# A new issue order for every engine of a one-core attention-plus-spectral-filter kernel

## The chip, the core and the metric

The kernel runs on one core of one Trainium2 chip. The metric is the device time of one execution in microseconds (us); lower is better. A core has five engines that run their own instruction streams and meet only at semaphores: TensorE (PE, matrix products into PSUM), VectorE (DVE), ScalarE (ACT), GpSimd (POOL) and SyncE (SP, which here only issues transfers). In the profile PEld is the loading of a matmul's stationary operand, a name ending in q is an engine's instruction queue.

## What is computed

Two token mixers over the same input, added under a gate per token. Branch A is attention in four segments of 512 tokens with a running memory; branch B is a filter in the frequency domain. Cut to what matters:

```python
B, S, D, H, N, L = 1, 2048, 640, 32, 4, 512        # head width Dh = 20
g = sigmoid((x * gate_w).sum(-1, keepdims=True))
q, k, v = x @ wq, x @ wk, x @ wv                    # as heads and segments
for s in range(N):
    p = softmax(qs @ ks.T * Dh**-0.5 + causal_mask)
    a_mem = (phi(qs) @ M) / (phi(qs) @ z + 1e-6)    # phi(t) = t+1 if t>0 else exp(t)
    out_s = gh * a_mem + (1 - gh) * (p @ vs)        # gh = sigmoid(beta), per head
    M, z = M + phi(ks).T @ vs, z + phi(ks).sum()
a = concat(out_s) @ wo
b = irfft2(rfft2(x) * (w_r + 1j * w_i))
return g * a + (1 - g) * b
```

## The kernel before

Everything is cut to 128 partitions. `record` writes the computation down as 2328 operations, each with what it reads and writes; a second table, `ORDER`, says in which order every engine issues them; `schedule` turns both into instruction streams and chooses buffers, and `emit` puts the waits in. One entry of `ORDER` holds an operation and the engine that does it:

```python
for v in order:
    o = ops[v // 2]
    o.eng = list(o.alts)[v % 2]
    queue[o.eng].append(o)
```

So an entry's half is the operation's number, and an odd entry takes the second of its two engines, where it has two. Each engine keeps its queue strictly: an instruction that waits holds up all that stand behind it on that engine. Which operation may run on which engine is fixed where it is recorded. Copies out of PSUM (`copy_alts`, L519) go to ScalarE or VectorE. [...] Products by the PSUM operand are VectorE's alone.

PSUM has eight banks. Four belong to the scores of attention (`qk`, one unit fills all four); the other four (`gen`) are handed round among all other matmul groups. A group takes a bank with its first matmul, and the bank is free for another when the operation that reads it out has ended. Since a group is often the fifth that wants one, a matmul often waits for an eviction.

The steps, with the lines they have in the profile:

- Opening. Transposed loads of x (`xt_load`, profile line L546), loads of the weights and of x in the filter's layout (L548). A first product of four heads (`proj_direct`) and the projections of q, k, v follow; all matmuls show as L514 (L512 where one product is split into four column groups). `fold` (L901, L906) adds and subtracts halves of x for the filter, on VectorE or GpSimd.
- Attention, segment by segment. `qk_unit` makes the scores, ScalarE takes their exponential (L1263, tile ex), GpSimd zeroes what the causal mask hides (L1284), a product with v follows. 80 such score units run one after the other through the whole kernel, and all other work lies between them.
- Memory. `phi` is made by L1072 (ACT) and L1084, L1085 (DVE); `mem_read_tile` divides the memory's answer (L1152, L1155, L1157; L1160 in the last segment).
- Filter. Products with tables, a product by the filter (L1439), sums (L1444), products back, and sums into the tile G (L1485).
- Denominators, for segments 0 to 2. `denominators` (L1202) reads the sums of the softmax back from DRAM, inverts them (L1211), multiplies them by the gate (L1213, tile rc), stores them (r_scr) and `finish_tile` loads them again spread over partitions (tile r), where five products with the attention output need them (L1526, `normal`, tile oU).
- Finish. Four tiles for each segment (`finish_tile`, L1506). For segments 1 and 2 the memory's part is loaded (tile mT, a transposing load) and added (L1534, `addmem`, 128x640). Then the filter's last product and the product with wo go into one bank, the bank is read out (L523 on ACT, L525 on DVE, tile ot) and stored.

TensorE works in three shapes: the full array; four row groups, for the scores (`qk`); four column groups, for half of the v products, the products of probabilities and v in segments 0 to 2, and the finish. A group of one shape that follows a group of another is called a change of shape below.

Of the kernel before, what the change touches and what calls it, by code (L numbers as in the profile page):

```python
# [461 lines left out]
class Kern:  # L462
# [79 lines left out]
    def dma(self, dst, src, nbytes, r, w, prio, tr=False, name="", after=(), queue="sp"):  # L542
# [37 lines left out]
        46, 0, 90, 26, 74, 23, 2, 4, 36, 24, 6, 8, 28, 10, 12, 72, 14, 16, 30, 18, 20, 178, 64, 34, 202, 66, 68, 44, 42, 70, 93, 214, 52, 190, 48, 94,  # L580
        204, 97, 216, 180, 192, 218, 104, 98, 182, 76, 206, 101, 194, 38, 208, 220, 196, 103, 198, 222, 201, 184, 224, 186, 210, 188, 296, 50, 212,
        256, 298, 362, 78, 300, 536, 32, 80, 274, 538, 258, 83, 302, 260, 262, 276, 130, 278, 264, 84, 54, 280, 106, 266, 282, 1904, 86, 304, 364,
        284, 88, 366, 108, 380, 306, 576, 132, 826, 268, 290, 828, 814, 110, 368, 578, 831, 816, 113, 382, 384, 386, 819, 370, 540, 388, 832, 270,
        834, 410, 412, 272, 836, 414, 416, 391, 418, 552, 372, 490, 420, 288, 492, 494, 114, 496, 498, 554, 118, 820, 822, 134, 336, 500, 240, 137,
        338, 242, 340, 120, 348, 58, 824, 342, 116, 350, 308, 122, 312, 544, 142, 226, 932, 546, 124, 344, 292, 244, 56, 228, 144, 246, 286, 248, 347,
        139, 352, 230, 294, 232, 126, 250, 354, 146, 234, 374, 1906, 149, 237, 1908, 356, 254, 1910, 359, 2094, 151, 238, 1912, 844, 1914, 252, 2124,
        140, 2126, 1916, 2128, 128, 2130, 360, 166, 2096, 40, 846, 2098, 154, 2132, 848, 2100, 2134, 1924, 326, 1926, 314, 2102, 168, 392, 1928, 2104,
        1930, 156, 892, 310, 1932, 152, 838, 1944, 1934, 170, 334, 1946, 158, 894, 840, 324, 316, 1948, 842, 808, 897, 161, 328, 810, 1950, 1952, 394,
        320, 813, 880, 886, 163, 882, 322, 1954, 888, 560, 332, 502, 884, 504, 396, 506, 330, 172, 508, 890, 448, 376, 510, 1936, 398, 450, 436, 512,
        438, 378, 402, 452, 514, 562, 440, 174, 442, 2162, 400, 1962, 2164, 176, 444, 2166, 516, 556, 454, 456, 2168, 446, 165, 2170, 458, 464, 460,  # L590
        466, 406, 1918, 468, 462, 470, 570, 472, 408, 2172, 910, 912, 542, 474, 898, 900, 318, 914, 602, 903, 2150, 548, 604, 2152, 2154, 2156, 2158,
        1920, 2178, 572, 404, 2160, 1966, 2180, 1958, 2182, 1922, 1968, 574, 904, 60, 2184, 2174, 2186, 906, 594, 2188, 1956, 564, 908, 1970, 2176,
        580, 934, 874, 596, 876, 1972, 879, 476, 566, 1974, 62, 478, 480, 550, 1977, 868, 870, 930, 422, 568, 482, 424, 873, 484, 426, 928, 916, 558,
        486, 428, 430, 488, 918, 2136, 432, 598, 2138, 920, 2140, 434, 2142, 856, 582, 858, 1960, 2144, 922, 519, 861, 924, 606, 584, 2146, 936, 1938,
        520, 2148, 926, 588, 523, 1020, 525, 608, 586, 652, 591, 2596, 802, 654, 862, 850, 804, 864, 852, 1940, 2216, 867, 2204, 2206, 2218, 2208,
        2220, 1942, 2210, 2222, 1980, 854, 2224, 2212, 656, 634, 2226, 2214, 1978, 778, 658, 2006, 2228, 636, 780, 2230, 2008, 1982, 2190, 2010, 782,
        2012, 526, 946, 2014, 786, 784, 2192, 948, 1964, 938, 940, 942, 2194, 788, 950, 2196, 945, 2198, 952, 600, 660, 2017, 2200, 790, 662, 2202,
        792, 2018, 976, 978, 1984, 794, 2020, 958, 798, 796, 1986, 960, 980, 954, 2233, 800, 1988, 982, 610, 956, 664, 2038, 612, 1990, 528, 2236,
        2234, 1992, 965, 530, 984, 986, 2040, 1995, 534, 2076, 988, 2078, 962, 2042, 1996, 2000, 1998, 2044, 991, 614, 618, 1016, 2080, 2024, 620,
        2002, 996, 1014, 2082, 2238, 638, 998, 2084, 972, 2004, 2022, 2046, 622, 668, 974, 992, 624, 2086, 2049, 2056, 626, 1018, 994, 1070, 1072,  # L600
        2058, 1074, 666, 2060, 1022, 1076, 642, 1002, 2050, 806, 1104, 1024, 1026, 670, 645, 1001, 2062, 532, 1028, 2270, 2064, 1031, 628, 2036, 2636,
        2252, 2240, 1106, 2272, 630, 2638, 2274, 2254, 640, 2066, 2276, 2106, 676, 616, 2640, 2256, 678, 592, 2258, 1010, 1004, 2243, 2026, 966, 968,
        2052, 2070, 2028, 1013, 632, 692, 971, 1006, 694, 680, 2244, 2642, 1009, 2644, 686, 1032, 2068, 1034, 682, 2246, 646, 1100, 2054, 2090, 1036,
        2030, 2088, 684, 2288, 649, 710, 2034, 2646, 672, 2290, 1039, 2566, 712, 674, 2292, 2598, 2294, 2600, 2306, 2072, 2602, 2110, 2604, 2308,
        2606, 2074, 2568, 2310, 700, 2092, 2108, 2312, 714, 2608, 726, 2112, 2786, 703, 716, 728, 2114, 1044, 2788, 2570, 688, 1062, 1064, 1046, 2790,
        696, 1066, 2792, 2794, 2650, 1069, 690, 1040, 2796, 650, 2574, 734, 1042, 1110, 698, 1078, 736, 1108, 1082, 730, 1080, 1112, 1114, 1118, 1102,
        1120, 732, 1122, 1116, 750, 1084, 1124, 2260, 2032, 738, 752, 2278, 1049, 2578, 2262, 2280, 2264, 2580, 2282, 704, 2266, 1051, 2284, 2268,
        2296, 2582, 744, 706, 1148, 1150, 2298, 718, 2586, 2648, 754, 2300, 1058, 720, 2302, 3288, 1152, 1089, 2616, 1061, 2618, 1126, 1155, 740,
        1130, 1052, 746, 1132, 1054, 2620, 2572, 1056, 2332, 1086, 1204, 1128, 748, 1206, 2334, 1208, 2622, 2624, 2250, 756, 1096, 1211, 1090, 1135,
        1192, 1092, 2627, 762, 2118, 1095, 2576, 2610, 2390, 1194, 1137, 1098, 1196, 765, 1198, 2392, 1200, 2314, 2120, 2698, 1203, 722, 2700, 2628,  # L610
        1138, 2316, 2702, 2318, 742, 1156, 2122, 1158, 2320, 1160, 1140, 724, 708, 1163, 2704, 2630, 2324, 2612, 2116, 1142, 1168, 2654, 2614, 2706,
        770, 2326, 1170, 1164, 758, 1166, 2842, 2844, 2846, 2848, 761, 2850, 2658, 2652, 2328, 2364, 2852, 766, 2676, 2330, 2366, 2709, 2678, 1280,
        2660, 2584, 2680, 2662, 2712, 2590, 1175, 2870, 2664, 1278, 2592, 2666, 2632, 2682, 2656, 2668, 2348, 1190, 2684, 2634, 2350, 2854, 2336,
        2710, 2856, 2858, 2860, 2862, 2672, 2286, 2896, 2687, 2898, 2864, 2358, 2340, 2866, 2872, 1274, 2352, 2868, 2342, 2874, 2876, 2360, 2882,
        2816, 768, 2884, 2818, 2362, 2878, 2820, 2688, 2886, 2880, 2888, 2822, 2890, 1188, 2692, 2824, 2690, 2900, 2344, 2826, 2902, 2904, 2670, 2382,
        2368, 2828, 2892, 2384, 2830, 2894, 2832, 2346, 2748, 2834, 2906, 2750, 1242, 2370, 1244, 1246, 2752, 2674, 2836, 2376, 2694, 1248, 2716,
        2838, 2696, 2448, 2714, 772, 2338, 2754, 2354, 2450, 2730, 2732, 2356, 2840, 2734, 2736, 2756, 1173, 2738, 2372, 2741, 2758, 2386, 2422, 2588,
        2378, 2375, 1144, 2760, 2394, 1176, 2742, 1147, 2768, 1186, 2770, 2424, 2718, 2772, 2322, 2774, 2802, 2776, 2744, 1178, 2764, 3290, 2779,
        2594, 1234, 3292, 1236, 774, 1238, 2798, 2762, 2746, 2406, 2782, 3328, 1276, 1241, 2408, 3294, 3296, 2766, 3298, 2720, 3330, 2780, 3301, 1182,
        2416, 2398, 1184, 3332, 1181, 2418, 2400, 1212, 2728, 3334, 2784, 3336, 1214, 2420, 1216, 2908, 2910, 2410, 1218, 3308, 3338, 2402, 2912,  # L620
        2440, 2800, 2404, 1254, 2442, 1250, 2426, 1256, 3310, 3312, 3314, 3316, 1252, 2428, 2914, 2916, 2412, 2434, 2918, 3318, 2804, 1366, 2498,
        1222, 2920, 1220, 1282, 2806, 2500, 2922, 2925, 1224, 2444, 1284, 2437, 3258, 2414, 1286, 3260, 1289, 1226, 2396, 1272, 1320, 1322, 3262,
        2927, 1290, 1292, 1229, 2304, 1324, 2388, 2506, 1326, 1294, 3266, 2952, 2508, 2380, 2446, 2962, 1297, 2430, 3320, 2954, 2964, 1259, 2956,
        2966, 3270, 3340, 2968, 3272, 2502, 2248, 2958, 3322, 1328, 2452, 2464, 3274, 2944, 2433, 2466, 1330, 2454, 3278, 2504, 3282, 2946, 1332,
        2948, 2456, 3284, 4010, 1334, 2468, 2950, 1298, 2458, 1260, 1362, 2980, 3350, 1300, 2470, 3352, 1302, 2474, 4008, 3354, 1304, 1230, 2476,
# [981 lines left out]
```

## Time and profile before

| | us |
|---|---|
| median of 13 runs | 244.34 |
| lowest, highest | 242.32, 245.25 |
| the profiled execution | 244.84 |
| its span, first to last instruction | 242.9 |
| mean granted TensorE clock | 0.993 of full |

| engine | busy us | share | instructions |
|---|---|---|---|
| PE | 227.3 | 94% | 4347 |
| ACT | 199.6 | 82% | 241 |
| DVE | 197.0 | 81% | 481 |
| POOL | 166.6 | 69% | 297 |

The profiled execution took 244.84 us, 1.9 more than its span, and 0.5 more than the median of the runs. Busy time of an engine is the time in which at least one of its instructions was under way; matmuls overlap, so PE's share says that it seldom stood still and not that it ran at its peak. The transfers moved 42.17 MB, 174 GB/s on the mean.

### The profile page before, as it was taken

The numbers are of one execution on the slowest core, as the hardware profiler recorded it, in microseconds if no ns is written. First come the engines' busy times: TensorE is split into PE (matmuls) and PEld (weight loads), VectorE is DVE, ScalarE is ACT, GpSimd is POOL, SyncE is SP. The second block draws the span as 40 slices with busy tenths as digits, with TensorE's granted clock in tenths as the row PEclk, the third lists the DMA queues.
The fourth block names the chain that finished last, engine by engine and source line by source line (L and its number), as shares of the span: only waits on it lengthen the run. The fifth ranks groups of instructions, "written<-read, shape, count | busy, mean of one in ns | idle before, by whom it ended". The sixth has DMA issues, their size and how long they took to land.

```text
span 242.9 us, 10242 instructions
## 1 busy us (share of the span) xinstructions
PE 227.3 (94%) x4347; PEld 141.2 (58%) x4361; DVE 197.0 (81%) x481; ACT 199.6 (82%) x241; POOL 166.6 (69%) x297
## 2 busy tenths in 40 slices
PE   7799999999999999999989999899989999799994
PEld 2575567665556565555546555455545557467794
DVE  0579998789899986997999798997988887736563
ACT  2189688799899999999989979999899978488730
POOL 8524268457969956947964999876899867559730
PEclk9999999999999999999999999999999999799999
DMA  7999849996996775494787572364776997642123
GB/s 171 279 363 213 227 123 165 268 205 148 244 233 155 169 227 144 106 232 92 237 205 236 167 217 66 101 171 139 189 217 200 221 198 83 125 71 85 57 86 108
DMA packets 58928, 42.17 MB, mean 174 GB/s; under 512 B 30020, under 2 KB 55172, under 8 KB 58884
## 3 DMA queue, kind: packets, MB, share of 16 engines
q1 hardware_dynamic: 57844, 40.96, 69.4%
q8 instruction: 34, 0.56, 1.0%
q10 hardware_dynamic: 1040, 0.57, 0.8%
q14 instruction: 10, 0.08, 0.1%
HBM read 23.32 MB, written 12.30 MB: 147 GB/s over the span
## 4 chain that ended last, share of the span: by engine, by line
PE 49%; DVE 20%; DMA 11%; ACT 9%; SPq 6%; issue 3%; ACTq 0%; DVEq 0%
PE psum L514 44%; ACT ex L1263 6%; PE psum L512 5%; SPq L548 3%; SPq L546 3%; DMA xsb<-in_A_x_dram 3%; DMA r_scr<-rc 3%; DMA qkp<-qk_scr 2%; DVE xf L901 2%; DVE xsb L906 2%; DMA qk_scr<-qu 2%; DVE Pt L1439 2%; DVE G L1485 1%; DVE va L1115 1%; DVE oU L1526 1%
## 5 line engine op out<-in xcount | busy, mean ns | idle before, releaser
L1263 ACT ACTIVATE ex<-psum 128x2048 bf16<-128x2048 f32 (+4 forms) x92 | 138.7, 1507 | 13.9 <-PE psum L514 12.3
L1284 POOL TENSOR_SCALAR_AFFINE_SELECT ex<-ex 128x256 bf16<-128x256 bf16 (+2 forms) x224 | 122.0, 567 | 40.0 <-ACT ex L1263 36.5
L514 PE MATMUL psum<-qkp 20*64 20x64 bf16 (+5 forms) x1280 | 32.6, 271 | 2.9 <-ACT ex L1263 1.9
L514 PE MATMUL psum<-xT,wk 128*128 128x256 bf16 (+1 forms) x280 | 34.0, 273 | 0.8 <-DMA wk<-in_A_wk_dram 0.6
L514 PE MATMUL psum<-wv,xT 128*32 128x321 bf16 (+3 forms) x400 | 30.0, 301 | 0.3 <-DVE va L1115 0.2
L514 PE MATMUL psum<-xT,wq 128*128 128x512 bf16 (+1 forms) x121 | 27.0, 380 | 1.5 <-DMA xT<-in_A_x_dram 0.8
L1439 DVE TENSOR_TENSOR Pt<-psum,Wt 128x642 bf16<-128x642 f32 x32 | 25.6, 822 | 2.3 <-PE psum L514 1.9
L514 PEld LDWEIGHTS psum<-qkp 20*64 20x64 bf16 x1280 | 13.5, 103 | 20.2 <-ACT ex L1263 13.5
L514 PEld LDWEIGHTS psum<-xT,wk 128*128 128x128 bf16 (+1 forms) x280 | 19.9, 97 | 6.9 <-DMA wk<-in_A_wk_dram 0.9
L512 PE MATMUL psum<-wo,oU 128*32 128x320 bf16 x480 | 22.7, 310 | 0.0
L906 POOL TENSOR_TENSOR xsb<-xf 128x320 bf16<-128x320 bf16 (+2 forms) x12 | 9.4, 788 | 16.7 <-DVE xsb L906 12.5
L525 DVE CAST ot<-psum 128x320 bf16<-128x320 f32 x21 | 10.1, 491 | 11.3 <-PE psum L512 8.9
L514 PEld LDWEIGHTS psum<-wv,xT 128*32 128x32 bf16 (+1 forms) x400 | 14.6, 96 | 7.9 <-issue 2.4
L1115 DVE TENSOR_TENSOR va<-psum,ebx 128x320 bf16<-128x320 f32 x32 | 15.2, 483 | 4.7 <-ACT gate L1113 2.4
L514 PE MATMUL psum<-big,Ac 128*128 128x160 bf16 (+2 forms) x96 | 18.1, 258 | 0.7 <-DVE Pt L1439 0.3
L514 PE MATMUL psum<-big,Cp 128*128 128x321 bf16 (+1 forms) x96 | 18.0, 302 | 0.2 <-DVE G L1485 0.2
L514 PE MATMUL psum<-ex,va 128*32 128x64 bf16 (+3 forms) x576 | 17.4, 256 | 0.7 <-DVE dn L1152 0.3
L1485 DVE TENSOR_TENSOR G<-eo,psum 128x320 bf16<-128x320 f32 x32 | 14.7, 482 | 3.6 <-PE psum L514 2.6
L514 PE MATMUL psum<-tt,Yt 128*128 128x256 bf16 (+1 forms) x96 | 16.4, 275 | 0.4 <-ACT qu L523 0.3
L514 PEld LDWEIGHTS psum<-ex,va 128*32 128x32 bf16 x576 | 11.0, 96 | 9.7 <-POOL ex L1284 3.4
L1072 ACT ACTIVATE et<-qu 128x512 bf16<-128x512 bf16 x25 | 15.6, 629 | 0.2
L512 PEld LDWEIGHTS psum<-wo,oU 128*32 128x32 bf16 x480 | 12.4, 99 | 4.8 <-issue 1.1
(99 smaller groups left out, 392.7 us busy)
## 6 DMA issues: line engine op xcount, KB each, us to landing
qkp<-qk_scr SPq DMA_DIRECT2D x28, 160.0 KB
tt<-tab_tt SPq DMA_DIRECT2D x8, 512.0 KB, 4.4
qk_scr<-qu SPq DMA_DIRECT2D x12, 256.0 KB, 3.6
u_scr<-ub SPq DMA_DIRECT2D x12, 256.0 KB, 3.6
xsb<-in_A_x_dram SPq DMA_DIRECT2D x8, 320.0 KB, 6.8
oU<-u_scr SPq DMA_DIRECT2D x15, 128.0 KB, 3.3
out_dram<-ot SPq DMA_DIRECT2D x12, 160.0 KB
Wt<-in_B_w_r_dram SPq DMA_DIRECT2D x16, 80.2 KB, 2.6
```

The source lines that it names most:

```text
L512: h = e.matmul(dst, wt, r_, start=st, stop=sp_, **{**kw, "tile_position": (0, q), "skip_group_check": True})
L514: h = e.matmul(o_, l_, r_, start=st, stop=sp_, **kw)
L525: alts["dve"] = (lambda e: e.tensor_copy(dst(), src()), 67 + 1.04 * n, 68.0)
L546: return e.dma_start_transpose(d_, s_)
L548: return e.dma_start(d_, s_)
L906: self.either(lambda e, dst=dst, src=src, d0=d0, n=n, op=op: e.tensor_tensor(xs.ap(o + dst, [D, 2], [1, n]), xf.ap(src + d0, [321, 2], [1, ...
L1072: self.one("act", lambda e: e.activation(et.ap(0, [1, L]), qsl(), ACT.Exp), L, [qb], [b("et", pi_)], late, name="phi_exp")
L1115: self.one("dve", lambda e: e.tensor_tensor(va.ap(i * H * VW + h0 * VW, [VW, nh], [1, DH]), self.ps(bank, 0, [DH, nh], [1, DH]), self.ebx. ...
L1263: self.one("act", lambda e, d=d, q=q: e.activation(self.ex.ap(*d), self.ps(bank, *q), ACT.Exp, scale=SC), n, [bank], [self.exb(s, 2 * pr + ...
L1284: self.one("pool", lambda e: e.affine_select(self.ex.ap(e0 + d0, [1280, 4], [1, n], np_=np_), self.ex.ap(e0 + s0, [1280, 4], [1, n], np_=np_),
L1439: self.one("dve", lambda e, ri=ri, Pt=Pt, Wt=Wt, wo_=wo_, bank=bank: e.tensor_tensor(Pt.ap(ri * 322, [644, 2], [1, KD]), self.ps(bank, 0, ...
L1485: self.one("dve", lambda e, q=q, n2=n2, bank=bank, eo=eo: e.tensor_tensor(self.G.ap(n2 * D + 639 * q, [1 - 2 * q, 320]), eo.ap(q, [1, 320] ...
```

## The change

Only the table `ORDER` differs; the operations, their buffers' sizes and the scheduler are the same. The first and the last rows of it:

```diff
     ORDER = (
-        46, 0, 90, 26, 74, 23, 2, 4, 36, 24, 6, 8, 28, 10, 12, 72, 14, 16, 30, 18, 20, 178, 64, 34, 202, 66, 68, 44, 42, 70, 93, 214, 52, 190, 48, 94,
-        204, 97, 216, 180, 192, 218, 104, 98, 182, 76, 206, 101, 194, 38, 208, 220, 196, 103, 198, 222, 201, 184, 224, 186, 210, 188, 296, 50, 212,
...
+        23, 0, 104, 24, 90, 72, 2, 26, 4, 6, 8, 28, 10, 12, 14, 74, 16, 46, 30, 202, 18, 34, 190, 44, 178, 20, 48, 180, 52, 192, 92, 42, 182, 95, 214,
+        194, 216, 204, 96, 218, 206, 36, 196, 208, 38, 198, 210, 201, 220, 212, 222, 184, 98, 186, 100, 188, 296, 32, 225, 103, 274, 298, 256, 76,
...
```

The built programs show what the new table moves. TensorE has the same 1073 matmul groups with the same 80 score units in the same sequence, the groups between them in a new one; changes of shape go from 229 to 241. Operations that change engine, net:

| operation | before | after |
|---|---|---|
| copies out of PSUM on ACT (L523) | 93 | 98 |
| of these the last ones (tile ot) | 11 | 17 |
| `fold` on POOL | 16 | 12 |
| `normal` on POOL (L1526) | 2 | 0 |
| `addmem` on POOL (L1330, L1534) | 5 | 2 |
| filter sums on POOL (L1444) | 16 | 15 |
| gate tables on POOL (L1022) | 2 | 4 |
| small gate operations on POOL | 11 | 15 |

Four places that the prediction speaks of, in the order of the built streams ("|" stands between instructions, numbers in brackets are operation numbers):

```
SP, opening
before  x part 1 | xT chunk 0 | beta | wk | xT chunks 1-2 | xT chunks 3-4 | wk rest | x part 0 | ...
after   wk | xT chunk 0 | xT chunks 1-2 | x part 1 | xT chunks 3-4 | wk rest | x part 0 | ...

DVE, memory read of segment 2
before  mem_den | gate | mem_rec | phi_max(1652) | mem_den | mem_rec | mem_mul(1493)
after   mem_den | mem_mul | mem_rec | W_mul | mem_mul(1493) | mem_den | mem_rec | phi_max(1652)

DVE, denominators of segment 2
before  ... sum, sum | gate table | sum, sum | L1211(1626) | normal, sum, sum | L1213(1627)
after   ... sum, sum | sum | last eviction | sum | L1211(1626) | L1213(1627)

finish of segment 2, its first tile: DVE  L1526 x5 | rs | addmem(2080) | rs | on(1915), in both
POOL beside it   before  addmem(2178), 128x640      after  addmem(2129), 128x640 | addmem(1865), 128x320
DVE further on   before  on | addmem(1865)          after  sum | addmem(2178)
```

## The prediction

> **What bounds the kernel now.** I read the page first (busy times, slices), then who waited for whom, the stretches of 1 us around the largest stop, and the timelines of the engines there.
>
> ```profile
> span 242.9 us, 10242 instructions
> PE 227.3 (94%) x4347; PEld 141.2 (58%) x4361; DVE 197.0 (81%) x481; ACT 199.6 (82%) x241; POOL 166.6 (69%) x297
> ...
> PEclk9999999999999999999999999999999999799999
> ```
>
> TensorE is the bound: it stands still for 242.9 - 227.3 = 15.6 us, of which 1.3 lie before its first matmul and 3.1 behind its last. Within the busy time lie the changes of shape. In the trace's list of weight loads, four-column groups of 320 columns start 136 ns apart; before a group of another shape the distance is 371, and that group's next follows after 15 instead of 136. A change of shape thus costs (371 - 136) - (136 - 15) = 114 ns, and 229 of them 26 us.
>
> ```profile
> PEld psum L514 <- ACT ex L1263: 13.5, 44, 0.8
> PEld psum L514 <- POOL ex L1284: 3.9, 12, 0.5
> PEld psum L514 <- DVE Pt L1439: 3.7, 15, 0.6
> ...
> PEld psum L514 <- DVE on L1325: 1.8, 1, 1.8
> PEld psum L514 <- DVE mem L1157: 1.8, 3, 1.3
> ```
>
> The columns are total, times, longest. Most stops are many and short: weight loads held until a score bank or a general bank is read out. They are spread over the kernel and no single edit takes them away. Two are long, the last two rows. The first of these, in stretches (busy PE, PEld, DVE, ACT, POOL; then the granted clock):
>
> ```profile
> 206.00:207.00 1.00, 0.69 (x28) 0.59 (x24) 0.96 (x4) 0.97 (x2) 0.79 (x1) 1.00 0.56 56
> 207.00:208.00 1.00, 0.00 (x0) 0.00 (x0) 1.00 (x2) 0.47 (x1) 0.60 (x1) 1.00 0.27 97
> ...
> 210.00:211.00 1.00, 1.00 (x20) 0.62 (x16) 0.47 (x1) 0.97 (x2) 0.68 (x3) 0.50 0.52 150
> ...
> 212.00:213.00 1.00, 1.00 (x22) 0.37 (x15) 0.85 (x3) 0.44 (x1) 0.00 (x0) 0.50 1.99 165
> ```
>
> TensorE stops at 206.7, goes on at 208.4, and from about 210 to 213 the granted clock is 0.50. Why it stopped, from three engines' timelines:
>
> ```profile
> 204.05 2.01 DVE L1526 TENSOR_TENSOR oU<-oU,r 128x512 bf16<-128x512 bf16 x5 [0.89 <-DMA r<-r_scr]
> 206.21 1.39 POOL L1534 TENSOR_TENSOR oU<-oU,mT 128x640 bf16<-128x640 bf16 x1 [0.74 <-DVE rs L1320]
> 206.35 1.60 DVE L1534 TENSOR_TENSOR oU<-oU,mT 128x640 bf16<-128x640 bf16 x1
> 208.40 0.32 PE L514 MATMUL psum<-G,fbg 128*32 128x320 bf16 x4 [1.71 <-DVE on L1325]
> ```
>
> VectorE waited 0.89 for the transfer of r; behind it in its queue stood five products, then addmem, then the eviction (on) that frees the bank. And addmem took 1.60 where the median of its kind is 0.48: GpSimd had begun its own addmem 0.14 earlier, and VectorE's ended soon after GpSimd's. The other long stop is alike, with GpSimd busy on masks without a gap:
>
> ```profile
> 122.34 1.43 DVE L1084 TENSOR_SCALAR phq<-qu 128x512 bf16<-128x512 bf16 x1
> 124.54 0.45 PE L514 MATMUL psum<-Bt,tt 128*128 128x321 bf16 x2 [1.02 <-DVE mem L1157]
> ...
> 6.57 0.62 PE L514 MATMUL psum<-xT,wk 128*32 128x256 bf16 x16 [0.40 <-DMA wk<-in_A_wk_dram]
> 8.03 0.40 PE L514 MATMUL psum<-xT,wq 128*32 128x512 bf16 x4 [0.84 <-DMA xT<-in_A_x_dram]
> ```
>
> The last two rows are the opening's waits for transfers.
>
> **The change, part by part.** The sum is made against the profiled execution, 244.84 us (span 242.9 and 1.9 around it), which lies 0.5 above the median of 244.34.
>
> (1) Changes of shape: 12 more x 0.114 = **+1.4**. They are covered only where TensorE would have waited anyway, so from 0 to +1.4; six lie in the stretch from 185 to 203, where it hardly waits, and I take the whole.
>
> (2) The stop at 206. VectorE makes L1213 directly behind L1211; the rows it stood behind are gone, and from the last sum before (185.6) to L1213 there is 6.4 us of VectorE's work instead of 8.5 (counts of the built order by the mean of each row), so the store of r can go 2.1 earlier. Behind L1213 stand 20 instructions of 9.0 us before the first product with r, against 18 of 8.0; r landed 9.5 after L1213 ended, so the wait for it shrinks from 0.89 to nothing or little. TensorE comes to this point 1.1 later (six changes of shape, three groups more). So the bank is free 2.1 + 1.1 = 3.2 earlier against TensorE's need, less 1.0 - 0.9 = 0.1 for the work added, and the stop was 1.7: **-1.7**, with 1.4 to spare. On SP the store of r is no longer behind five loads of oU and a second load of mT, but behind two loads of oU, one of qkp and a store of ot. If it lands later by more than the spare, the stop returns: 0 to -1.7.
>
> GpSimd's addmem beside VectorE's is now number 2129, whose mT is issued directly behind r. By the median landing of mT, 5.0 us, against 2.4 for r and 2.0 for the five products, it starts some 1.2 after them, when VectorE's addmem (0.16 + 0.48) is through. It can still meet VectorE's second addmem (2178), behind the eviction that TensorE needs. What would be late then is the next two evictions, by up to 1.1.
>
> (3) The clock. At 0.50 from 210 to 213.1, TensorE lost about half of 3.2 us: **-1.6** if there is no stop long enough, 0 if there is.
>
> [...]
>
> (4) The stop at 124: the eviction L1157 (1493) now stands ahead of the product of phi that took 1.43. From L1152 to its end I count 0.49 + 0.25 + 0.82 + 0.43 = 2.0 us, before 2.7: -0.7, of which I take **-0.5**, since another bank may be asked for at once; bounds 0 and -1.0.
>
> (5) Opening: on SP wk and the second piece of xT come ahead of x's first part and beta, whose issue took 0.41 + 0.57. The waits were 0.40 + 0.84 = 1.24; I take **-0.6**, bounds 0 and -1.24. The first fold waits longer for its x instead; VectorE has 2.8 us of idle time between 10 and 15.
>
> (6) Four folds go from GpSimd to VectorE, +1.2 us there (rows of 0.33 to 0.51), in a stretch where it is busy 5.00 of 5.00 (15 to 35 us). TensorE waits little for it there: **+0.6**, bounds 0 and +1.2.
>
> (7) Six last evictions go to ScalarE, +6 x 0.44 = 2.6 us, from 190 on. It is at 4.6 of 5 us until 195 and at 2.8 to 4.6 after; TensorE's own work hides them: 0. With that cover gone each delays a bank by 0.44.
>
> (8) All other groups are dealt anew. Some 35 short waits of 0.2 to 0.6 may grow or shrink; the old order was free of the worst of them in this trace, the new one need not be. I take one new wait of median size, **+0.4**, bounds -1.5 and +2.5.
>
> Sum: 1.4 - 1.7 - 1.6 - 0.5 - 0.6 + 0.6 + 0.4 = -2.0, and 244.84 - 2.0 = **242.8 us**.
>
> **Rivals.** A, the stop is only halved: VectorE's addmem runs freely (-1.1), but r is still waited for, TensorE stands for 0.6 and the clock falls all the same. 244.84 + 1.4 - 1.1 - 0.5 - 0.6 + 0.6 + 0.4 = 245.0, no change. For it: the clock fell after a stop of only 1.71. Against it: the spare of 1.4.
>
> B, r lands late (slower): the store of r took 6.98 us from issue to the load behind it (194.65 to 201.63), with 0.8 MB of wo in the queue ahead, and wo is now closer ahead of it. From 1.4 us later than it came before, measured from L1213, TensorE stops again; at 3.1 the whole stop is back, and the clock falls. Then 1.4 - 0.5 - 0.6 + 0.6 + 0.4 = +1.3: 246.1. Against it: fewer bytes stand between.
>
> C, the collision moves: GpSimd's addmem (2129) still starts first, because mT lands in 3.9 (the shortest seen) and VectorE's products run late. [...]
>
> D, the scattered waits (8) at their upper bound instead of 0.4: 242.8 + 2.1 = 244.9, no change; above that, slower, where TensorE's 15.6 us of standing still grow by more than 2.5 (a sixth).
>
> **How the numbers follow.** No change means within 0.5%, 243.1 to 245.6, about what a measurement of this kernel can tell. The forecast, faster: 0.48, by itself 241.2 to 243.1. A, C and the lower half of D: 0.22. B, 0.17, and D beyond its bound, 0.13, slower: 0.30. For 8 in 10 the range leaves out a tenth on each side: down to 241.0, where (5), (4) and (1) take their better bounds in part, and up to 246.4, just above B.
>
> **What would show it.** Right: changes of shape unnoticed outside TensorE's busy time (PE busy up by about 1); no PE stop over 1 us between 200 and 212 and the clock at 1.00 there; addmem of VectorE at 0.5; PE's wait for wk and xT under 0.7 in total. Wrong: a granted clock of 0.50 anywhere after 10 us, VectorE waiting for r by more than 1 us, or PE's stops above 14 us in sum.

## The result and the profile after

| | before | after |
|---|---|---|
| median, us | 244.27 (48 runs) | 248.25 (11 runs) |
| lowest, highest | 242.32, 248.35 | 245.29, 249.83 |
| ratio to before | 1 | 1.0142, interval 1.0109 to 1.0174 |
| profiled execution (span) | 244.84 (242.9) | 247.04 (245.1) |

The new order is slower by 1.4%, about 3.5 us. The forecast was 2.0 faster. The profiled execution of after lies 1.2 below its own median, so the trace shows 2.2 of the difference and says nothing of the rest. Of the 68 runs of the kernel before that stood beside the experiments, the 22 with a mean clock of at least 0.997 have a median of 242.4, the other 46, with 0.986 to 0.993, of 244.5.

The page of after, its busy times and the slices of the granted clock:

```profile
span 245.1 us, 10264 instructions
PE 228.6 (93%) x4349; PEld 141.5 (58%) x4361; DVE 195.9 (80%) x480; ACT 201.8 (82%) x246; POOL 164.2 (67%) x293
...
PEclk9999999999999999999999999999999999799999
```

TensorE works 1.3 longer than before, as more changes of shape would have it, and stands still for 245.1 - 228.6 = 16.5 instead of 15.6. The slice with a 7 is still there. Who held up the weight loads (total, times, longest):

```profile
PEld psum L514 <- ACT ex L1263: 12.0, 38, 0.8
PEld psum L514 <- POOL ex L1284: 6.3, 15, 1.3
PEld psum L514 <- DVE va L1115: 3.0, 7, 1.7
PEld psum L514 <- DVE Pt L1439: 2.4, 10, 0.3
...
PEld psum L514 <- POOL Mz L1361: 1.7, 2, 1.3
...
PEld psum L514 <- DVE on L1325: 1.3, 1, 1.3
```

The row of the stop at 124, L1157, is gone from the top. The many short waits for scores and for the filter (L1263, L1439) are smaller in sum, those for masks (L1284) larger. But the stop for L1325 is still there, and there are three new long ones: 1.7 under L1115, 1.3 under L1284 and 1.3 under L1361. First the old one, from the timelines of VectorE, SP and TensorE:

```profile
205.99 1.09 DVE L1526 TENSOR_TENSOR oU<-oU,r 128x512 bf16<-128x512 bf16 x3
208.81 0.76 DVE L1526 TENSOR_TENSOR oU<-oU,r 128x512 bf16<-128x512 bf16 x2 [1.74 <-DMA oU<-u_scr]
209.61 0.49 DVE L1534 TENSOR_TENSOR oU<-oU,mT 128x640 bf16<-128x640 bf16 x1
210.30 0.49 DVE L1325 TENSOR_TENSOR on<-psum,rs 128x320 bf16<-128x320 f32 x1
...
202.36 0.51 SPq L548 DMA_DIRECT2D r<-r_scr  x1
202.92 1.96 SPq L546 DMA_TRANSPOSE mT<-o_scr  x1
204.92 0.60 SPq L548 DMA_DIRECT2D oU<-u_scr  x1
...
210.84 0.32 PE L514 MATMUL psum<-G,fbg 128*32 128x320 bf16 x4 [1.05 <-DVE on L1325]
```

VectorE no longer waits for r, and addmem takes 0.49: both as forecast. It waits 1.74 for another transfer instead, a load of oU. SP issues it at 204.92, behind the load of r and the issue of a transposing load of mT that took 1.96; it is 3.9 from issue to landing, and the third product ended at 207.07. 204.92 + 3.9 - 207.07 = 1.75, the wait. Behind it stands the same eviction (1915, L1325) as before, and TensorE stops for 1.05. The stretches there (busy PE, PEld, DVE, ACT, POOL; then the clock):

```profile
210.00:211.00 1.00, 0.16 (x8) 0.13 (x11) 0.97 (x4) 0.53 (x2) 1.00 (x1) 1.00 0.13 46
211.00:212.00 1.00, 1.00 (x48) 0.62 (x44) 1.00 (x3) 0.00 (x0) 1.00 (x2) 0.91 0.59 116
212.00:213.00 1.00, 1.00 (x20) 0.57 (x23) 0.93 (x4) 0.88 (x2) 0.93 (x3) 0.50 0.51 78
```

So the half clock came back too.

That addmem runs freely has another reason than the one that the prediction gave. VectorE's reciprocal in before, then GpSimd's addmem and VectorE's reciprocal in after:

```profile
206.18 0.25 DVE L1323 RECIPROCAL rs<-rs 128x16 f32<-128x16 f32 x1
...
209.72 1.63 POOL L1534 TENSOR_TENSOR oU<-oU,mT 128x640 bf16<-128x640 bf16 x1 [3.66 <-DVE rs L1320]
210.02 0.24 DVE L1323 RECIPROCAL rs<-rs 128x16 f32<-128x16 f32 x1
```

In both traces GpSimd's addmem is released by VectorE's first instruction on rs (L1320), not by the landing of mT. In before VectorE makes both instructions on rs (L1320, L1323) ahead of its addmem, which then begins 0.14 behind GpSimd's; in after addmem stands between the two and begins 0.11 ahead of GpSimd's. So the stream "rs | addmem(2080) | rs | on(1915)", shown above for both kernels, is that of after alone.

The three new stops, from the timelines (VectorE, then GpSimd where it is shown, then TensorE):

```profile
37.06 2.51 DVE L906 TENSOR_TENSOR xsb<-xf 128x318 bf16<-128x318 bf16 x2
36.73 4.51 POOL L1284 TENSOR_SCALAR_AFFINE_SELECT ex<-ex 64x512 bf16<-64x512 bf16 x8
40.02 0.28 PE L514 MATMUL psum<-fcat,xsb 128*128 128x128 bf16 x2 [1.36 <-DVE va L1115]
...
62.87 1.15 DVE L1444 TENSOR_TENSOR Yt<-Pt 128x321 bf16<-128x321 bf16 x2
63.94 0.68 DVE L525 CAST ub<-psum 128x512 bf16<-128x512 f32 x1
64.76 0.33 PE L514 MATMUL psum<-Mz,phq 128*128 128x154 bf16 x3 [0.99 <-DVE ub L525]
...
101.28 1.76 DVE L1085 TENSOR_TENSOR phk<-phk,et 128x512 bf16<-128x512 bf16 x2
102.96 0.78 DVE L1444 TENSOR_TENSOR Yt<-Pt 128x321 bf16<-128x321 bf16 x1
103.66 0.51 DVE L525 CAST Bt<-psum 128x322 bf16<-128x322 f32 x1
104.32 0.73 PE L514 MATMUL psum<-ex,va 128*32 128x512 bf16 x24 [1.03 <-DVE Bt L525]
```

At 38 VectorE makes a fold (82) that GpSimd made before; the second of the two folds takes 2.08, where a fold takes some 0.32 undisturbed, beside GpSimd's masks that follow each other without a gap. At 63 and 103 an eviction (L525) stands behind products of two SBUF tensors that were slowed in the same way (L1444 0.53 to 0.78, where its mean in before is 0.35; L1085 0.65 and 1.19, there 0.49); in the rows above, of the weight loads, the same two stops go under L1284 and L1361, whose instruction came last by the profile. At 103 the eviction (624, tile Bt) was ScalarE's before and is VectorE's now.

To add up small stops, I take for each score unit the start of its weight loads, less the time that the columns of all matmuls before it take to stream (in both traces matmuls of 256 columns start 109 ns apart in the median and those of 512 columns 216: 0.42 ns a column) and 0.114 for each change of shape before it. What is left is the lag of TensorE at that unit, in us, with the changes of shape taken out:

| at score unit | before | after | e1 | e9 | e2 | e10 |
|---|---|---|---|---|---|---|
| 1 | 3.11 | 2.67 | 1.98 | 2.13 | 2.99 | 3.07 |
| 25 | 7.48 | 8.11 | 7.76 | 7.07 | 6.60 | 6.54 |
| 29 | 7.52 | 9.71 | 9.37 | 7.62 | 6.64 | 6.58 |
| 33 | 7.80 | 10.07 | 9.74 | 8.46 | 7.06 | 6.85 |
| 41 | 11.15 | 12.86 | 13.08 | 11.24 | 10.41 | 9.79 |
| 69 | 17.13 | 18.53 | 18.95 | 16.91 | 16.40 | 15.75 |
| 77 | 20.88 | 21.63 | 19.48 | 17.32 | 17.70 | 16.39 |
| last group | 20.68 | 21.55 | 19.41 | 17.25 | 17.50 | 16.19 |

Before and after differ by 0.87 at the end, and with 12 x 0.114 = 1.37 by the 2.2 of the two traces. Up to unit 29 after loses 2.2, at the stop at 124 (units 33 to 41) it gains 0.56, and from 69 to 77, where 3.3 were to be won, 0.65. The other columns are experiments of the next section.

### The profile page after: what moved, and what is told of

It reads as the page before. It is cut to its first block, busy times and chain, and to the rows that moved or that the text cites. A ratio compares the mean times of both kernels' runs of the same rounds, so it can differ in the third digit from the quotient of the medians.

```text
span 245.1 us, 10264 instructions
## 1 busy us (share of the span) xinstructions
PE 228.6 (93%) x4349; PEld 141.5 (58%) x4361; DVE 195.9 (80%) x480; ACT 201.8 (82%) x246; POOL 164.2 (67%) x293
## 4 chain that ended last, share of the span: by engine, by line
PE 54%; DVE 17%; ACT 16%; DMA 6%; issue 3%; SPq 2%; POOL 1%; DVEq 0%
PE psum L514 48%; ACT ex L1263 12%; PE psum L512 6%; DMA wk<-in_A_wk_dram 2%; DMA mT<-o_scr 2%; DVE Pt L1439 2%; ACT et L1072 2%; SPq L546 2%; DMA oU<-u_scr 2%; DVE G L1485 2%; DVE va L1115 1%; DVE Yt L1444 1%; DVE phk L1085 1%; DVE Cp L525 1%; DVE phq L1084 1%
## 5 line engine op out<-in xcount | busy, mean ns | idle before, releaser
L1263 ACT ACTIVATE ex<-psum 128x2048 bf16<-128x2048 f32 (+4 forms) x92 | 138.8, 1509 | 15.4 <-PE psum L514 13.4
L1284 POOL TENSOR_SCALAR_AFFINE_SELECT ex<-ex 128x256 bf16<-128x256 bf16 (+2 forms) x224 | 122.4, 568 | 39.2 <-ACT ex L1263 36.0
L514 PE MATMUL psum<-wv,xT 128*32 128x321 bf16 (+3 forms) x400 | 31.1, 302 | 0.0
L514 PE MATMUL psum<-xT,wq 128*128 128x512 bf16 (+1 forms) x123 | 28.2, 391 | 1.2 <-DVE va L1115 0.8
L1439 DVE TENSOR_TENSOR Pt<-psum,Wt 128x642 bf16<-128x642 f32 x32 | 25.4, 819 | 2.7 <-PE psum L514 2.6
L1115 DVE TENSOR_TENSOR va<-psum,ebx 128x320 bf16<-128x320 f32 x32 | 15.3, 485 | 6.0 <-PE psum L514 3.4
L525 DVE CAST ot<-psum 128x320 bf16<-128x320 f32 x15 | 7.3, 490 | 12.1 <-PE psum L512 8.7
L514 PE MATMUL psum<-big,Ac 128*128 128x321 bf16 (+2 forms) x96 | 16.6, 257 | 0.0
L514 PEld LDWEIGHTS psum<-xT,wq 128*128 128x128 bf16 (+1 forms) x135 | 9.8, 99 | 8.6 <-issue 1.8
```

The costliest lines, as they stand in the source:

```text
L514: h = e.matmul(o_, l_, r_, start=st, stop=sp_, **kw)
L525: alts["dve"] = (lambda e: e.tensor_copy(dst(), src()), 67 + 1.04 * n, 68.0)
L1115: self.one("dve", lambda e: e.tensor_tensor(va.ap(i * H * VW + h0 * VW, [VW, nh], [1, DH]), self.ps(bank, 0, [DH, nh], [1, DH]), self.ebx. ...
L1263: self.one("act", lambda e, d=d, q=q: e.activation(self.ex.ap(*d), self.ps(bank, *q), ACT.Exp, scale=SC), n, [bank], [self.exb(s, 2 * pr + ...
L1284: self.one("pool", lambda e: e.affine_select(self.ex.ap(e0 + d0, [1280, 4], [1, n], np_=np_), self.ex.ap(e0 + s0, [1280, 4], [1, n], np_=np_),
L1439: self.one("dve", lambda e, ri=ri, Pt=Pt, Wt=Wt, wo_=wo_, bank=bank: e.tensor_tensor(Pt.ap(ri * 322, [644, 2], [1, KD]), self.ps(bank, 0, ...
```

## The experiments

Each kernel is one of the two with single entries of `ORDER` moved. The diffs show the moved instructions in the stream of their engine, "|" between instructions, operation numbers in brackets.

### e1: the load of oU ahead of r again

```diff
 SP, after's order
-oU | oU | r(2068) | mT | oU(2077) | mT
+oU | oU | oU(2077) | r(2068) | mT | mT
```

> The new order, with one load moved on SP: the fifth load of oU of segment 2 goes ahead of the load of r and of the transposing load of mT behind it, instead of after both. Theory L (the stop at 209 to 211 of the new order is this load, 1.74 us of VectorE's waiting): the wait goes to under 0.4 us, TensorE does not stop there for more than 0.5, the granted clock stays 1.00 in 205 to 220, and the time falls by 1.0 for the stop and up to 1.5 for the clock, ratio to the kernel before 1.004 to 1.010 instead of 1.014. Rival P (the stop is set by the eviction's place behind five products and an addmem, whichever transfer is late): the stop stays above 0.8 us and the clock at 0.50, ratio 1.014.

Measured: 245.18 (244.24 to 248.21), ratio 1.004 (1.0003 to 1.0076), against 1.0142 for after: 1.0% or 2.4 us from one load, with an interval of 0.3 to 0.4% on either side of both ratios. Timelines of VectorE, SP and TensorE:

```profile
206.40 1.75 DVE L1526 TENSOR_TENSOR oU<-oU,r 128x512 bf16<-128x512 bf16 x5
...
200.77 1.86 SPq L548 DMA_DIRECT2D oU<-u_scr  x3
203.03 0.51 SPq L548 DMA_DIRECT2D r<-r_scr  x1
...
210.03 0.31 PE L514 MATMUL psum<-G,fbg 128*32 128x320 bf16 x4
```

The five products run without a break and TensorE's row has no wait. The clock stays at 1.00 over the whole execution, and the lag grows by 0.53 from unit 69 to 77, against 3.10 in after. With the late load moved, stop and half clock are gone, and nothing else was changed; rival P is out. How firmly the clock hangs on the stop, the last section takes up.

### e2: the old order with its addmem on VectorE

```diff
 DVE, before's order
-on(1915)
+on(1915) | addmem(2178)
 POOL, before's order
-addmem(2178)
```

> The order before, with one addition (addmem 2178, 128x640) taken from GpSimd to VectorE, behind the eviction that TensorE needs. My step (2) of the prediction: VectorE's own addmem runs in 0.5 instead of 1.6, the stop at 206 shrinks from 1.7 to about 0.6. If the clock falls only after the longer stop, it stays 1.00 and the time falls by 1.1 + 1.6, ratio 0.989; if it falls all the same, ratio 0.995. Rival (the stop costs nothing that is not waited for later): ratio 1.000.

Measured: 242.0 (241.44 to 242.88), ratio 0.9881 (0.9844 to 0.9919). From VectorE's timeline and that of the weight loads:

```profile
205.25 0.43 DVE L1534 TENSOR_TENSOR oU<-oU,mT 128x640 bf16<-128x640 bf16 x1
...
206.12 0.10 PEld L514 LDWEIGHTS psum<-G,fbg 128*32 128x32 bf16 x4 [0.38 <-DVE on L1325]
```

The addmem that took 1.60 takes 0.43, the weight loads stop for 0.38 instead of 1.8, and the lag from 69 to the end grows by 1.10 instead of 3.55. So the collision with GpSimd's addmem was the cause of the old stop, as the prediction read it, and one entry takes it away. By its ratio e2 is faster than both kernels. Much of this is the clock: all four runs of e2 have a mean clock of at least 0.997, and the four such runs of before beside them have a median of 243.1.

### e3 to e6: where the new order loses

The same operations, with one table up to a point of time on TensorE and the other one from there; this point is called the join below. e6 has after's order everywhere but on SP, which keeps before's.

```diff
 ORDER
-after
+before up to 48 us, then after           (e3)
+before up to 185 us, then after          (e4)
+before up to 112 us, then after          (e5)
+after, SP's operations as before has them (e6)
```

> The order before up to where its TensorE is at 48 us, the new order for the rest. Theory O (the new order loses in the opening, where a fold on VectorE took 2.08 us beside GpSimd's masks and TensorE stopped 1.65): the time falls by 0.8 to 1.7 against the new order, ratio 1.007 to 1.011. Rival S (the loss is spread over the later stages): ratio stays at 1.012 to 1.016.

> The order before up to where its TensorE is at 185 us, the new order for the rest, so the new finish alone. The new finish has 7 changes of shape more (0.8 us) and the stop with the late load of oU. Theory S (the loss is spread over the stages before): ratio 0.998 to 1.004. Rival F (the finish is what loses): ratio 1.010 to 1.016.

> The order before up to where its TensorE is at 112 us, the new order for the rest. The new order to 48 cost nothing, and its part from 185 on cost nothing against the old one, so its loss of 1.4% lies between 48 and 185. [...] Rival N (it lies from 112 to 185): ratio 1.010 to 1.016.

> The new order on PE, DVE, ACT and POOL, the old order of SP's transfers. Theory L (of SP's queue only the late load of oU costs): as with that load moved alone, ratio 1.000 to 1.007, no TensorE stop above 0.5 us between 206 and 214. Rival Q (the new SP queue costs or gains in other places too, wk and xT first in the opening among them): ratio under 0.997 or above 1.010; by step (5) of the prediction the old queue in the opening costs 0.4 to 0.6 us, so 1.006 to 1.010 if nothing else differs.

| | median | ratio |
|---|---|---|
| e3 | 248.25 | 1.0148 (1.0085 to 1.0212) |
| e4 | 245.03 | 0.9997 (0.9956 to 1.0039) |
| e5 | 248.46 | 1.0141 (1.0103 to 1.0178) |
| e6 | 253.05 | 1.0357 (1.0303 to 1.0412) |

e3: with the old opening the median is that of after, but the interval also reaches into the range of theory O (1.007 to 1.011), so that it doesn't tell whether the opening costs anything. In its profile score unit 1 starts 1.1 us behind after's, unit 9 starts 0.5 ahead of it, and from unit 25 on they start 0.2 behind again: of the 1.6 won in the opening, 0.7 are lost again behind the join. e4: the new finish behind the old order neither gains nor loses. Its profiled execution (248.12) has a stop at the join itself: the units start 1.7 later than before's from unit 9 up to unit 65 and 6.3 later at unit 67. So this bounds the finish from one side only. e5, which was to tell whether the loss lies ahead of 112 or behind it, fails as a test for the same reason: the lag grows by 5.8 between units 33 and 37, at the join. It still shows the stop at 103 gone (0.04 from 25 to 29, after 1.60), since that stretch is the old one. e6 lies above 1.010, where rival Q has it, but not for a reason that Q names: from unit 59 to 63 its units fall from 3.1 to 9.3 behind after's, with a stop of 3.61 in the matmuls at 182, where the old queue of SP and the new order of computing don't fit. What it shows is that SP's order can't be judged apart from the order of the others.

### e7: the price of a change of shape

```diff
 PE, e2's order, from 218 to 228 us
-wo x4 | wo x4 | wo x4 | va,ex x40
+va,ex x4 | wo x4 | va,ex x8 | wo x4 | va,ex x12 | wo x4 | va,ex x16
...
```

The same in two other places there, 16 changes more in sum.

> The order before with addmem 2178 on VectorE (ratio 0.988), and in the finish, from 220 to 231 us, eight column-group products put between the products of probabilities and v, which makes 16 changes of shape more and nothing else. Theory: each costs 0.114 us, nothing covers it there: +1.8 us, ratio 0.994 to 0.998, and TensorE's time from score unit 73 to the last weight load goes up by 1.8. Rival (a change costs nothing where weight loads run ahead): ratio 0.988.

Measured: 243.71, ratio 0.9985 (0.9935 to 1.0034), against 0.9881 for e2. From score unit 77 to the last group, all at full clock in both profiles, it is 20.51 us instead of 18.86: 1.65 for 16, 0.103 each. The price of 0.114 holds within a tenth. The profile has a fall of the clock to 0.50 ahead of that stretch, at 209, which the last section takes up.

### e8 and e9: two of the new stops

```diff
 e8 = e1, and
 DVE
-sum | Bt(624) | eviction
+sum | eviction
 ACT
-gate | exp
+gate | exp | Bt(624)
 e9 = e8, and
 DVE
-fold | fold(82) | va
+fold | va
 POOL
-mask | mask
+mask | fold(82) | mask
```

> The new order with the load of oU ahead (ratio 1.004) and one eviction (624) given back from VectorE to ScalarE, where the old order had it. Theory M: the stop of 1.14 us at 103 goes, the time falls by 0.8 to 1.2 us more, ratio 0.999 to 1.001. Rival (the stop moves to the next bank, or ScalarE's exponentials come 0.5 later instead): ratio 1.003 to 1.006.

> The new order with the load of oU ahead, the eviction 624 on ScalarE (ratio 1.002 with these two) and one fold (82) given back from VectorE to GpSimd, before the run of masks that held it up for 1.76 us. Step (6) of the prediction, mis-sized: TensorE's stop of 1.65 us at 38 goes, the time falls by 0.8 to 1.5 us, ratio 0.996 to 0.999. Rival (GpSimd's masks come 0.8 later instead and the stop moves there): ratio 1.000 to 1.003.

e8: 244.41 (243.21 to 248.06), ratio 1.0017 (0.9981 to 1.0054). ScalarE's timeline and that of the weight loads:

```profile
101.39 0.54 ACT L523 ACTIVATE Bt<-psum 128x322 bf16<-128x322 f32 x1
...
104.05 0.61 PEld L514 LDWEIGHTS psum<-ex,va 128*32 128x32 bf16 x24 [0.21 <-issue]
```

The eviction starts at 101.39, in after at 103.66, and the stop is gone: from unit 25 to 29 the lag grows by 0.56 instead of 1.60. Of this 0.46 comes back up to unit 33 (0.82 instead of 0.36), so the rival is right in part, and 0.6 are kept, as the ratios have it (1.004 and 1.0017); their intervals overlap.

e9: 243.19 (242.84 to 244.92), ratio 1.0021 (0.9987 to 1.0055). VectorE's, GpSimd's timeline:

```profile
36.55 0.52 DVE L906 TENSOR_TENSOR xsb<-xf 128x318 bf16<-128x318 bf16 x1
...
36.12 0.75 POOL L906 TENSOR_TENSOR xsb<-xf 128x318 bf16<-128x318 bf16 x1
```

The fold takes 0.75 on GpSimd instead of 2.08 on VectorE, and from unit 5 to 9 the lag grows by 0.90 (after, e1 and e8: 1.85 to 1.86). The ratio doesn't show it and misses the expected 0.996 to 0.999: the kernel before ran at 243.54 beside e9 and at 244.39 beside e8. By the ratio e9 is no different from e8 or from before.

### e10 and e11: the old order repaired twice, and the new opening

```diff
 e10 = e2, and
 DVE
-mem_rec | phi_max(1652) | mem_den | mem_rec | mem_mul(1493)
+mem_rec | mem_den | mem_rec | mem_mul(1493) | phi_max(1652)
 e11 = e10, and
 SP, the first transfers
-x part 1 | xT chunk 0 | beta | wk | xT chunks 1-2
+wk | xT chunk 0 | xT chunks 1-2 | x part 1
```

> The order before with addmem 2178 on VectorE (ratio 0.988), and the product of phi that took 1.43 us put behind the eviction 1493, as in the new order. Step (4): TensorE's stop at 124 shrinks from 1.0 by 0.5 to 0.9 us, ratio 0.984 to 0.987. Rival (the next bank is waited for instead): ratio 0.988.

> As the run before it, with SP's first fifteen transfers in the new order's sequence but for beta, which stays fourth: wk and the two first pieces of xT ahead of x. Step (5): TensorE's first score unit starts 0.3 to 1.0 earlier; if that lasts, the time falls by 0.3 to 0.6 us, ratio lower by 0.001 to 0.0025. Rival (VectorE's folds set the opening, TensorE loses the lead again by 35 us): no change.

e10: 241.8 (239.99 to 244.12), ratio 0.9947 (0.9916 to 0.9978). The expected ratio is missed, though no kernel here has lower times: beside it the kernel before was at 243.54, beside e2 at 244.77, so the two ratios can't be set against each other. In the trace the part of step (4) is there: the lag from unit 33 to 41 grows by 2.94 instead of e2's 3.35. By its ratio e10 beats both kernels, with two entries moved; against the 15 runs of before beside it with a mean clock of at least 0.997 (median 242.4) it gains 0.6.

e11: 242.47 (241.44 to 244.73), ratio 0.9968 (0.9935 to 1.0001). No gain. In its profile the first score unit starts at 13.99, in e10's at 13.06; but eight profiles with before's whole opening have it from 12.87 to 14.01 and four with after's from 12.21 to 13.42, so a single one decides nothing.

### e12: the late load put into the old order

```diff
 SP, e2's order
-oU(2077) well ahead of r(2068)
+r(2068) | out | oU(2077)
```

> The order before with addmem 2178 on VectorE (ratio 0.988), and the load of oU (2077) put behind the load of r and a store on SP, about as late as the new order has it. Theory L: VectorE waits for it by 1 to 2 us behind r, TensorE stops again for over 1 us near 207 and the granted clock falls to 0.50 for some 3 us: ratio 0.994 to 1.002. Rival P (r sets the stop, the load is hidden): ratio 0.988.

Measured: ten runs from 240.71 to 249.24, ratio 0.9937 (0.9891 to 0.9983) of the seven below 244: just under theory L's range and above rival P's 0.988, with an interval that reaches into the one and nearly to the other. In the three above 246 the mean clock is 0.985 to 0.993, in the other seven at least 0.998. The profiled one is of the three (246.42). SP's, VectorE's and TensorE's timeline:

```profile
202.11 0.56 SPq L548 DMA_DIRECT2D r<-r_scr  x1
203.37 0.53 SPq L548 DMA_DIRECT2D oU<-u_scr  x1
...
207.51 1.43 DVE L1526 TENSOR_TENSOR oU<-oU,r 128x512 bf16<-128x512 bf16 x4 [2.37 <-DMA oU<-u_scr]
...
210.10 0.32 PE L514 MATMUL psum<-G,fbg 128*32 128x320 bf16 x4 [2.48 <-DVE on L1325]
```

The stop that e2 had taken away is back, longer than before, and by the wait that after has: VectorE 2.37 for the load, TensorE 2.48 for L1325. So the late load can make the stop in the other order too; that is shown for this one execution. What it costs e12 doesn't tell, since the seven shorter runs (median 241.5) show no loss against e10, which ran beside them without the late load, and none of them was profiled. The load is issued 1.3 behind r here and 2.6 in after, so that its landing may still have been in time there.

## Why the prediction was wrong

**Steps (2) and (3), -3.3 forecast, 0.65 came (units 69 to 77).** The reading of the old stop was right: e2 takes the collision away, with a ratio of 0.988; in e1, where nothing is late, the lag grows by 0.53 from unit 69 to 77 against 3.75 before, which is 3.2 of the forecast 3.3. What failed is the sentence on SP, "the store of r is no longer behind five loads of oU and a second load of mT, but behind two loads of oU". I counted what the store of r had been freed from and didn't ask where those loads had gone: one of them went behind r and mT, and one of the same five products, the fourth in VectorE's queue, needs it. The trace of before had all that was needed: its 15 loads of oU land 3.3 after their issue in the median, and SP issues the transposing loads of mT for 1.2 to 1.6. Behind r's 0.5 and mT's 1.2 the fifth load lands 0.5 + 1.2 + 3.3 = 5.0 after r's issue; r itself lands after 2.4, three products of 0.4 end at 3.6: a wait of 1.4, and 1.74 came, with the issue of 1.96 and the landing of 3.9. Rival B had this mechanism, a late transfer ahead of the products, for the transfer of r; at its place stood oU. e1 puts 2.4 us on it, stop and clock together.

That VectorE's addmem ran in 0.49 was luck as far as the reason goes. Step (2) had GpSimd's addmem wait for mT and start 1.2 behind the products; it started some 0.15 behind them, released by VectorE's rs, and VectorE's came first by 0.11, in after, e1, e8 and e9 alike, because it now stands ahead of a reciprocal that the prediction didn't see moved.

**Step (8), +0.4, and (6), +0.6: mis-sized.** "One new wait of median size" were two long stops, at 63 and 103, and the folds made a third at 38. The trace has after 2.2 behind before at unit 29. I had read in the trace of before that a VectorE instruction with its operands in SBUF took longer beside GpSimd's (phi 1.43 instead of 0.28 at 122 beside masks, addmem 1.60 instead of 0.48 at 206 beside addmem) and used it for the two places that the change frees, not for those that it makes: the four folds and every eviction that now stands behind such an instruction. A fold was priced at its undisturbed 0.33 to 0.51; beside masks it took 2.08. e9 shows the fold's own repair worth 0.95 of lag at its place, e8 the eviction's 0.6. The stop at 63 wasn't repaired and isn't priced.

**Step (1), +1.4: right.** PE busy rose by 1.3, and e7 has 0.103 for each change.

**Step (4), -0.5: right.** From unit 33 to 41 the lag grows by 2.79 instead of 3.35, -0.56; e10 with that entry alone has -0.41 against e2.

**Step (5), -0.6: not settled.** The weight loads' waits for wk and xT did go, but one for wq (1.2) came; the matmuls still wait 0.37 for xT and 0.53 for wk, 0.90 in total, where under 0.70 was the sign of being right. The lag at the first unit is 0.44 lower, its start 0.2 earlier, within the scatter that e11 shows.

**Step (7), 0: right.** From unit 77 to the end the lag falls by 0.08, before by 0.20. The eviction that did harm, 624, went the other way, from ScalarE to VectorE, and the net numbers of the change hid it.

**The sum.** By the lag, forecast and trace differ by 4.2: 2.65 in steps (2) and (3) and 1.8 up to unit 29 (steps (5), (6) and (8): +0.4 forecast, 2.19 came), less 0.3 from unit 41 to 69, of which no step spoke. With three entries repaired (e9) the median is 243.19 and the profiled execution 242.84; that this meets the forecast of 242.8 is chance, for against the runs of before beside it, 243.54, it is no gain that can be told, and it is 0.8 above those 15 of them with a mean clock of at least 0.997. The forecast was made against a profiled execution with the half clock, which by the clocks above is not in every run. In the same runs e10 has 241.8, 1.39 below e9, as much as the 12 changes of shape cost (1.37); by the profiled executions it is 2.6, so that this may be chance. Left open are the 1.2 by which after's runs exceed its trace; the half clock can't be their cause alone, for the five of its twelve runs with a mean clock of at least 0.997 have a median of 247.3.

## What to carry to other kernels

When a store or load is moved ahead in an in-order queue, list where each transfer that it overtook now stands and which instruction needs it: the queue's gain for one operand is another's delay, and a consumer waits for the last of them. Where the trace shows an engine's instructions slowed beside another's (here a fold at 2.08 instead of some 0.32), price an instruction that moves there by the slowed row wherever the other engine is busy without gaps, and look at what stands behind it, evictions above all. Read the operations that change engine one by one, not as net counts, and where instructions of two engines slow each other, look at which instruction releases each of them.

## What was not expected of the hardware

**The clock.** In before it fell to 0.50 after a stop of 1.71 in the matmuls, in after behind one of 1.05, but not behind the longer one of 1.36 at 39. The stretch there in after:

```profile
39.00:40.00 1.00, 0.00 (x0) 0.00 (x0) 1.00 (x3) 0.06 (x1) 1.00 (x2) 1.00 1.18 353
40.00:41.00 1.00, 0.97 (x21) 0.70 (x21) 0.86 (x2) 0.40 (x1) 0.93 (x3) 1.00 0.68 205
```

TensorE does nothing for a whole us, and the clock stays at 1.00. The length of a stop alone doesn't tell whether the clock falls. Nor was a long stop needed: in e7's profile, with a mean clock of 0.991, the clock is at 0.50 from 209.2 to 212.6, and in the 3.4 us before that the matmuls stood still for 0.45 and 0.59 at the longest. In the traces' record of the clock the half clock lasts 3.41 us in before (209.74 to 213.15) and in after (211.82 to 215.23), and by the stretches of e12 3.4; ahead of it the record has 204.80 us of full clock in before and in after alike, though the stops ahead of it differ. What sets the moment of the fall, no run here shows. But the falls are more frequent where the stop is: the mean clock is at least 0.997 in 22 of 68 runs of before and 5 of 12 of after, whose profiles have the stop at 207 or 210, and in 28 of 28 of e2, e10 and e11 and 28 of 30 of e1, e8 and e9, whose profiles don't.

**VectorE beside GpSimd.** The fold that took 2.08 in after (37.49 to 39.57) ran beside five masks without a gap between them, the longest of 0.79. So it was held up through more than one of GpSimd's instructions.
